# An inverse table permuted so that result stores take every third partition, and loads of a second transform ordered behind the chunks' transfers

## The chip, the core and the metric

The kernel runs on one core of one Trainium2 chip. TensorE (PE) multiplies matrices into PSUM, VectorE (DVE), ScalarE (ACT) and GpSimd (POOL) work on tiles in SBUF, whose first axis is the partition (0 to 127), and SyncE (SP) issues nearly all DMA transfers between SBUF and DRAM. Each engine takes its instructions in the order in which they were queued. The metric is the device time of one execution in microseconds, as the median of several runs.

## The reference

The input is x of shape (2, 3136, 256). Three blocks follow each other:

```
...
    X = np.fft.rfft(x, axis=1)
    Yr = Xr @ w_r - Xi @ w_i + b_r
    Yi = Xr @ w_i + Xi @ w_r + b_i
    Yr = np.sign(Yr) * np.maximum(np.abs(Yr) - lam, 0.0)   # Yi the same
    y = np.fft.irfft(Y, n=x.shape[1], axis=1)
...
    ch = np.maximum(xn @ w_ch1, 0.0) @ w_ch2               # xn: x normalised per row
    x = x + ch
...
    u = x + real(fft(fft(x, axis=1), axis=2))
    out = u + np.maximum(un @ w_ch1, 0.0) @ w_ch2          # un: u normalised per row
```

## The kernel before

The 3136 rows of a batch are split as 49 x 64 (n1 x n2), so that each Fourier transform along the rows is a 49-point one, a twiddled 64-point one, and back. The kernel has four stages.

The first transform, its mixing with w_r and w_i, the shrinking and the inverse 64-point part run as steps over both batches (`p2_b`, `p2_mix`, `p2_inv`). The result lies in `yg[b]`, one tile per batch with 128 partitions of 32 KB. Class `Inverse` does the inverse 49-point part with the table `cim`: `quad` (L336) multiplies with it, and the result is written back into `yg[b]`, with n1 as the partition, channel half h in partitions 64h to 64h + 48. `store(c)` writes it to DRAM (`dY`), rows n1 = 16c to 16c + 15 of each half in one DMA of 512 KB, 16 partitions of 32 KB; c = 3 is the one row left, n1 = 48. For batch 0 the order is: store piece 0, load the first two chunks' rows from dY, store pieces 1 to 3. For batch 1, pieces 0 and 1 are queued behind a transfer of the fourth chunk, and 2 and 3 behind one of the fifth (`store3`).

Then come 13 chunks of up to 512 rows of the first two-layer block (`mlp1`), and 13 of the second (`mlp2`), in `run_mlp`. A chunk's rows are fetched (L657), their mean and variance taken, normalised, turned in two steps by DVE (`flip`, L710) and a round trip through DRAM (dT<-q at L716, then `land`, q<-dT at L724), split by ACT and DVE or POOL into a high and a low part in tile u0r (`trans`), and multiplied: `l1` (PE L217 to L219, ACT L771, DVE L773), `l2` (PE L792 and L793, DVE adds L798 and L799), `store` (L808). The first two chunks are turned on PE instead (L748, then ACT L751). The tile u0r lies where `yg[0]` lay, so its first write waits until `yg[0]` has been stored. The first layer's matmuls, the second layer's and the other stages' all stand in one order on PE.

The transform along the rows for the third block (`Stage98`, "second transform") runs between the chunks, in eight steps per batch: batch 0 in chunks 8 to 10 of mlp1, batch 1 in chunks 1 to 3 of mlp2. `start` loads what the middle channel needs and the first two pieces, `ahead` a third, each of the first five steps one more. A piece is two DMAs of 256 KB (L398, u0r<-dX), written into a ring of four buffers; POOL folds it for batch 1 (L410 to L412), `quad` multiplies, ACT copies, SP stores it (dA<-o).

The order of instructions on each engine comes from a planner, which places them by modelled times and dependencies; the position in the source gives the priority. `tc.issue_after(ins)` adds the rule that what is traced inside it stands behind `ins` on `ins`'s engine. It orders and adds no semaphore.

Of the kernel before, what the change touches and what calls it, by code (L numbers as in the profile page):

```python
# [67 lines left out]
def _tables():  # L68


    t = {}

    def ang(num, den):
        return 2.0 * np.pi * (np.asarray(num, np.int64) % den) / den

    n1 = np.arange(N1)
    ca = np.zeros((NQ, NQ))
    cam = np.zeros((NQ, 4, 32))
    cim = np.zeros((4, 32, 64))

    for s in range(2):
        for k1 in range(1, NK + 1):
            a = ang(n1 * k1, N1)
            q = 4 * (k1 - 1) + s
            ca[2 * n1 + s, q] = np.cos(a)
            ca[2 * n1 + s, q + 2] = -np.sin(a)
            cam[2 * n1 + s, 2 * s, k1] = np.cos(a)
            cam[2 * n1 + s, 2 * s + 1, k1] = -np.sin(a)
            cim[2 * s, k1, n1] = np.cos(a)
            cim[2 * s + 1, k1, n1] = -np.sin(a)  # L90
        ca[2 * n1 + s, 96 + s] = 1.0
        cam[2 * n1 + s, 2 * s, 0] = 1.0
        cim[2 * s, 0, n1] = 1.0
    cs = ca.copy()
    for q in range(0, 96, 4):
        cs[:, q:q + 2], cs[:, q + 2:q + 4] = -ca[:, q + 2:q + 4], ca[:, q:q + 2]
    cq = np.zeros((128, 128))
    for s in range(2):
        cq[64 * s:64 * s + N1, 0:N1], cq[64 * s:64 * s + N1, 64:64 + N1] = ca[s::2, s::2], cs[s::2, s::2]
    t["ca"] = cq  # L100
    t["cam"] = cam.reshape(NQ, 128)
    t["cim"] = cim.reshape(128, 64)

    n2 = np.arange(N2)[:, None]
    k2 = np.arange(N2)[None, :]
    cb = np.zeros((2, N2, NK + 1, 128))
    ci = np.zeros((2, N2, NK, 2, N2))
    sg = np.where(np.arange(N2) >= 32, -1.0, 1.0)[None, :]
    for k1 in range(0, NK + 1):
        a = ang(n2 * (k1 + N1 * k2), N)  # L110
        c, s = np.cos(a), np.sin(a)
        re = np.stack([c, s])
        im = np.stack([-s, c])
        cb[:, :, k1, 0:32] = im[:, :, 32:]
        cb[:, :, k1, 32:96] = re
        cb[:, :, k1, 96:128] = im[:, :, :32]
        if k1:
            f = 2.0 / N
            ci[0, :, k1 - 1, 0] = f * c.T
            ci[1, :, k1 - 1, 0] = -f * (s * sg).T  # L120
            ci[0, :, k1 - 1, 1] = f * s.T
            ci[1, :, k1 - 1, 1] = f * (c * sg).T
    cb[:, :, 1:] = cb[:, :, 1:].reshape(2, 2, 32, NK, 128).swapaxes(0, 1).reshape(2, N2, NK, 128)
    t["cb"] = cb.reshape(128, (NK + 1) * 128)
    t["ci"] = ci.reshape(128, NK, 2, 2, 32).swapaxes(2, 3).reshape(128, NK * 128)

    kk = np.arange(33)[None, :]
    a = ang(n2 * (N1 * kk), N)
    cb0 = np.zeros((N2, 102))
    ci0 = np.zeros((68, N2))  # L130
    cb0[:, 0:33] = np.sin(a)
    cb0[:, 34:67] = np.cos(a)
    cb0[:, 68:101] = -np.sin(a)
    t["cb0"] = np.stack([cb0.reshape(2, 32, 102), np.zeros((2, 32, 102))], 1).reshape(128, 102)
    w = np.full((33, 1), 2.0 / N)
    w[0] = w[32] = 1.0 / N
    ci0[0:33] = w * np.cos(a).T
    wi = w.copy()
    wi[0] = wi[32] = 0.0
    ci0[34:67] = -wi * np.sin(a).T  # L140
    t["ci0"] = np.stack([ci0.reshape(68, 2, 32), np.zeros((68, 2, 32))], 2).reshape(68, 128)

    c = np.arange(D // 2)[:, None]
    kd = np.arange(129)[None, :]
    a = ang(c * kd, D)
    cd = np.stack([np.cos(a), np.sin(a)], 1)
    cd[0, 1, 0], cd[0, 1, 128] = 1.0, -1.0
    cd[1:, 1, 0] = cd[1:, 1, 128] = 0.0
    t["cd"] = cd.reshape(D // 2, 2 * 129)
    t["ident"] = np.eye(128)  # L150
    ident = t.pop("ident")
    out = {"ident": ident.astype(np.float32)}
    for k in ("ca", "cam", "cim", "cb", "ci", "cb0", "ci0", "cd"):
        out[k] = t.pop(k).astype(np.float32)
    assert not t
    return out
# [3 lines left out]
def fourier_moe_kernel(ctx, tc, x, w_r, w_i, b_r, b_i, g_ln, w11, w12, w21, w22,  # L160
                       t_ca, t_cam, t_cim, t_cb, t_ci, t_cb0, t_ci0, t_cd, t_ident, out):
    nc = tc.nc
    sp = nc.sync
# [37 lines left out]
    def v_copy(o, i):  # L201
        nc.vector.tensor_copy(o, i)

    mark, tab = {}, {}

    def sub(eng, o, a, b):
        ins = eng.tensor_tensor(out=o, in0=a, in1=b, op=ALU.subtract)
# [56 lines left out]
    yg = [cp.tile([128, 2, 32, 128], F32, tag=f"u{b}", name=f"yg{b}") for b in range(NB)]  # L264
# [23 lines left out]
    class Forward:  # L288
# [8 lines left out]
        def load(self, k, cut=1):  # L297
            t = self.slot()[0:NQ]
            w = 1024 // cut
            for e in range(cut):  # L300
                ins = sp.dma_start(out=t[:, e * w:(e + 1) * w],
                                   in_=x[self.b, k][:, e * w:(e + 1) * w])
                mark["sp"] = getattr(ins, "ins", ins)
            self.raw[k] = t
# [44 lines left out]
    class Inverse:  # L349
# [24 lines left out]
        def store(self, c):  # L374
            n0, n1 = 16 * c, min(16 * c + 16, N1)
            for h in range(2):
                v = yg[self.b][64 * h + n0:64 * h + n1].rearrange("p s j c -> p (s j c)")
                o = dY[self.b][h].rearrange("(n s) f -> n (s f)", s=2)[n0:n1]
                sp.dma_start(out=o, in_=v)

    class Stage98:
# [10 lines left out]
        def load(self):  # L392
            g = self.nl
            if g >= 8:
                return
            t = next(s98_ring)
            for s in range(2):
                sp.dma_start(out=t[64 * s:64 * s + 64], in_=self.src[s][:, g * 1024:(g + 1) * 1024])  # L398
            self.raw[g] = [t[:, e * 512:(e + 1) * 512] for e in range(2)]
            self.nl += 1  # L400

# [227 lines left out]
    class Chunk:  # L629
# [15 lines left out]
        def fetch(self):  # L645
            y = next(y_ring)
            if self.front is None:
                self.y = y.rearrange("p (h i c) -> p i h c", h=2, c=128)
            else:
                self.y = y.rearrange("p (i c) -> p i c", c=D)  # L650
            for ps_, i, n, ap in self.loads:
                if self.front is None:
                    o = y.rearrange("p (h i c) -> p h i c", h=2, c=128)[ps_, :, i:i + n, :]
                else:
                    o = self.y[ps_, i:i + n, :]
                    o = o if n > 1 else o[:, 0, :]
                ins = sp.dma_start(out=o, in_=ap)  # L657
                self.got = getattr(ins, "ins", ins)

        def like(self, a):  # L660
            return a if self.front is not None else a.rearrange("p (h c) -> p h c", h=2)
# [42 lines left out]
        def flip(self, h):  # L704

            x = self.nt * 32
            if h == 0:
                self.z = q_tiles[1]
            z = self.z[:, h * 4 * x:(h + 1) * 4 * x]
            nc.vector.transpose(out=z.rearrange("p (j i t) -> p i j t", j=4, t=32),  # L710
                                in_=self.yn[:, 0:self.nt, h * 128:(h + 1) * 128]
                                .rearrange("p i (j c) -> p i j c", j=4))
            if h == 0:
                return
            d = next(dT_ring).rearrange("h f -> (h f)")[0:1024 * x]
            ins = sp.dma_start(out=d.rearrange("(h p f) -> p h f", h=2, p=128),  # L716
                               in_=self.z[:, 0:8 * x].rearrange("p (h f) -> p h f", h=2))
            self.trip = getattr(ins, "ins", ins)
            self.d = d

        def land(self):
            x, d = self.nt * 32, self.d
            self.xt = q_tiles[2]
            ins = sp.dma_start(out=self.xt[:, 0:8 * x].rearrange("p (i x) -> p i x", i=8),  # L724
                               in_=bass.AP(d.tensor, d.offset, [[x, 128], [128 * x, 8], [1, x]]))
            self.trip = getattr(ins, "ins", ins)

        def trans(self, c):
            nt = self.nt
# [71 lines left out]
        def store(self, last):  # L801

            for ps_, i, n, ap in self.stores:
                if i + n - 1 != last:
                    continue
                s = self.o[ps_, i:i + n, :]
                eng = nc.scalar if self is mlp2[-1] and ps_.start == 64 else sp
                ins = eng.dma_start(out=ap, in_=s if n > 1 else s[:, 0, :])  # L808
                self.sent = getattr(ins, "ins", ins)

    ALLP = slice(0, 128)

# [230 lines left out]
    for i in range(NS + INV_BEHIND):  # L1043
# [6 lines left out]
        at = [inv0 if 2 * i + d in range(2 * STAGE3_FROM + 2, 2 * STAGE3_FROM + 10) else None for d in range(2)]  # L1050
# [37 lines left out]
    def run_mlp(chunks, nxt, hooks):  # L1088

        allc = chunks + nxt  # L1090
        for k, ch in enumerate(chunks):
# [17 lines left out]
            if n is not None and n.flipped:  # L1109
                if not n.landed:  # L1110
                    put(LAND_AT, land, n, allc[k - 1].sent if k else None)
                for c in range(2):
                    put(("l2", 0), split, c)
# [183 lines left out]
```

## Time and profile before

| | us |
|---|---|
| median of 3 runs | 799.08 (798.7 to 799.92) |
| the profiled execution | 795.47 |
| its span, first to last instruction | 793.7 |
| PE busy | 772.1 (97%) |
| DVE busy | 547.2 (69%) |
| ACT busy | 360.2 (45%) |
| POOL busy | 104.6 (13%) |

The profile is of one execution. Busy times of engines overlap, and the busy time of PE includes time at a lower clock. Of the 101.02 MB that DMA moves, 100.18 go through the one queue that SP feeds.

### The profile page before, as it was taken

How to read it: one execution, taken by the hardware profiler on the slowest of the kernel's cores; microseconds unless marked ns; L12 is line 12 of the kernel's file. 1: busy time of each engine (PE TensorE's matmuls, PEld its weight loads, DVE VectorE, ACT ScalarE, POOL GpSimd, SP SyncE). 2: the span in 40 equal slices, each digit the busy share in tenths (PEclk: the TensorE clock that was granted, in tenths of full speed). 3: DMA queues.
4: the chain of work that ended last, by engine and by line, in shares of the span. 5: the costliest groups of instructions: out<-in, count | busy, mean ns of one | idle time of the engine just before them, and what ended most of it. 6: DMA issues, size and time to landing. Idle time of an engine off the chain costs nothing.

```text
span 793.7 us, 12217 instructions
## 1 busy us (share of the span) xinstructions
PE 772.1 (97%) x4396; PEld 642.5 (81%) x4396; DVE 547.2 (69%) x1253; ACT 360.2 (45%) x791; POOL 104.6 (13%) x113
## 2 busy tenths in 40 slices
PE   9999999989999899999999999969999999999997
PEld 3989978966688789987778988757788898888887
DVE  6899986876755888867776766537556757666643
ACT  0553366356662444646443344346444435444421
POOL 0564312330110111100000001324100000000000
PEclk9999999999999999999999999989999999999999
DMA  8852204633087323495853227665543343322211
GB/s 244 247 184 111 81 1 54 163 111 107 27 222 189 105 92 107 153 222 160 264 171 99 88 85 172 179 178 156 151 137 92 107 124 121 109 70 73 62 34 40
DMA packets 84706, 101.02 MB, mean 127 GB/s; under 512 B 20306, under 2 KB 63036, under 8 KB 84450
## 3 DMA queue, kind: packets, MB, share of 16 engines
q1 hardware_dynamic: 84566, 100.18, 44.5%
q8 instruction: 35, 0.57, 0.3%
q14 instruction: 25, 0.20, 0.1%
q10 hardware_dynamic: 80, 0.07, 0.0%
HBM read 60.76 MB, written 41.42 MB: 129 GB/s over the span
## 4 chain that ended last, share of the span: by engine, by line
PE 83%; DMA 8%; DVE 5%; issue 1%; ACT 1%; SPq 1%; POOL 0%; ACTq 0%; DVEq 0%; POOLq 0%
PE psb L792 22%; PE psa L217 12%; PE psb L793 11%; PE psa L219 11%; PE psa L218 11%; PE psc L336 4%; PE psb L517 4%; DMA q<-dT 4%; DMA dY<-yg 3%; PE psc L862 3%; PE psa L484 1%; PE psc L887 1%; PE psa L323 1%; PE psc L539 1%; DVE yg L325 1%
## 5 line engine op out<-in xcount | busy, mean ns | idle before, releaser
L771 ACT ACTIVATE h<-psa 128x512 fp32r<-128x512 f32 (+2 forms) x208 | 117.9, 573 | 213.2 <-PE psa L219 160.4
L773 DVE SCALAR_TENSOR_TENSOR h<-psa,h 128x512 fp32r<-128x512 f32 (+2 forms) x208 | 135.0, 654 | 64.6 <-ACT h L771 60.7
L792 PE MATMUL psb<-r2b,h 128*128 128x512 f32 x392 | 138.1, 400 | 7.4 <-DVE o L799 7.4
L792 PE MATMUL psb<-r3a,h 128*128 128x512 f32 x392 | 137.7, 397 | 0.0
L793 PE MATMUL psb<-r3a,h 128*128 128x256 f32 x392 | 106.5, 280 | 0.0
L793 PE MATMUL psb<-r2b,h 128*128 128x256 f32 x392 | 106.4, 282 | 0.0
L792 PEld LDWEIGHTS psb<-r2b,h 128*128 128x128 f32 x392 | 72.6, 190 | 23.4 <-issue 8.2
L792 PEld LDWEIGHTS psb<-r3a,h 128*128 128x128 f32 x392 | 72.1, 188 | 21.0 <-issue 5.7
L217 PE MATMUL psa<-u0r,r3a 128*128 128x512 f32 (+1 forms) x208 | 81.4, 391 | 5.4 <-ACT u0r L199 3.4
L517 PE MATMUL psb<-wm,h 128*128 128x256 f32 (+1 forms) x600 | 84.4, 290 | 0.0
L217 PE MATMUL psa<-u0r,r2b 128*128 128x512 f32 (+2 forms) x208 | 82.0, 394 | 1.3 <-ACT u0r L199 1.3
L517 PEld LDWEIGHTS psb<-wm,h 128*128 128x128 f32 (+1 forms) x600 | 76.6, 188 | 5.0 <-issue 3.2
L218 PE MATMUL psa<-u0r,r3a 128*128 128x512 f32 (+1 forms) x208 | 79.4, 382 | 0.0
L218 PE MATMUL psa<-u0r,r2b 128*128 128x512 f32 (+2 forms) x208 | 78.7, 378 | 0.0
L219 PE MATMUL psa<-u0r,r2b 128*128 128x512 f32 (+2 forms) x208 | 78.3, 381 | 0.0
L793 PEld LDWEIGHTS psb<-r2b,h 128*128 128x128 f32 x392 | 74.8, 191 | 3.1
L219 PE MATMUL psa<-u0r,r3a 128*128 128x512 f32 (+1 forms) x208 | 76.7, 380 | 0.1
L793 PEld LDWEIGHTS psb<-r3a,h 128*128 128x128 f32 x392 | 73.9, 189 | 2.6
L798 DVE TENSOR_TENSOR o<-psb,yb 128x256 f32<-128x256 f32 x74 | 30.2, 421 | 65.5 <-PE psb L793 65.3
L199 ACT ACTIVATE yg<-psc 128x512 f32<-128x512 f32 (+1 forms) x58 | 48.2, 870 | 42.5 <-PE psc L539 28.0
L217 PEld LDWEIGHTS psa<-u0r,r3a 128*128 128x128 f32 x208 | 39.5, 190 | 19.6 <-issue 5.7
L217 PEld LDWEIGHTS psa<-u0r,r2b 128*128 128x128 f32 x208 | 39.1, 188 | 13.1 <-issue 5.7
(119 smaller groups left out, 1193.4 us busy)
## 6 DMA issues: line engine op xcount, KB each, us to landing
dT<-q SPq DMA_DIRECT2D x19, 512.0 KB
q<-dT SPq DMA_DIRECT2D x19, 512.0 KB
s<-in_moe_w_ch_dram SPq DMA_DIRECT2D x16, 512.0 KB
u0r<-dX SPq DMA_DIRECT2D x32, 256.0 KB
dA<-o SPq DMA_DIRECT2D x64, 128.0 KB
dY<-yg SPq DMA_DIRECT2D x12, 512.0 KB
r<-dA SPq DMA_DIRECT2D x48, 128.0 KB
dX<-o SPq DMA_DIRECT2D x10, 512.0 KB
```

The source lines that it names most:

```text
L199: nc.scalar.activation(out=o, in_=i, func=AF.Copy, scale=scale)
L217: nc.tensor.matmul(out=ps, lhsT=lh, rhs=rh, start=first, stop=False)
L218: nc.tensor.matmul(out=ps, lhsT=ll, rhs=rh, start=False, stop=False)
L219: ins = nc.tensor.matmul(out=ps, lhsT=lh, rhs=rl, start=False, stop=last)
L336: ins = nc.tensor.matmul(out=ps[s][64 * e:64 * e + 64, 0:n], lhsT=w[64 * s:64 * s + k], rhs=v[e][64 * s:64 * s + k], start=True, stop=True)
L517: ins = nc.tensor.matmul(out=ps[0:m, u * D:(u + 1) * D], lhsT=xv[:, o:o + m], rhs=wm_hl[wv][:, e, c, :], start=k == 0, stop=k == 11)
L771: ins = nc.scalar.activation(out=h[:, 0:n], in_=ps[:, 0:n], func=AF.Relu)
L773: ins = nc.vector.scalar_tensor_tensor(out=l[:, 0:n], in0=ps[:, 0:n], scalar=0.0, in1=h[:, 0:n], op0=ALU.max, op1=ALU.subtract)
L792: nc.tensor.matmul(out=ps, lhsT=h[:, ts_], rhs=w2[:, f, :], start=f == 0, stop=False)
L793: ins = nc.tensor.matmul(out=ps[:, 0:D], lhsT=l[:, ts_], rhs=w2[:, f, 0:D], start=False, stop=f == NF - 1)
L798: nc.vector.tensor_tensor(out=self.like(o), in0=self.like(ps[:, 0:D]), in1=self.y[:, i], op=ALU.add)
L862: nc.tensor.matmul(out=ps, lhsT=self.raw[p][0:n, k, q * 128:(q + 1) * 128], rhs=self.cols(n, pr[k][1], im), start=True, stop=True)
```

## The change

The table `cim` gets its columns in another order. Column `at` holds n1: n1 = 0 to 15 go to columns 0, 3, 6, ..., 45, the next 16 to 1, 4, ..., 46, the next to 2, 5, ..., 47, and n1 = 48 stays. The partition of the result is the column of the table, so `store(c)` now reads partitions c, c + 3, ..., 16 of them; DRAM gets the same rows at the same places. Besides, a dictionary `spx` remembers the last DMA of the chunks that was traced on SP (fetch, dT<-q, q<-dT, output store), and the loads of the second transform are traced behind it.

```diff
@@ _tables
+    at = np.where(n1 < 48, n1 % 16 * 3 + n1 // 16, n1)
...
-            cim[2 * s, k1, n1] = np.cos(a)
-            cim[2 * s + 1, k1, n1] = -np.sin(a)
+            cim[2 * s, k1, at] = np.cos(a)
+            cim[2 * s + 1, k1, at] = -np.sin(a)
...
-        cim[2 * s, 0, n1] = 1.0
+        cim[2 * s, 0, at] = 1.0
@@ fourier_moe_kernel
-    mark, tab = {}, {}
+    mark, tab, spx = {}, {}, {}
@@ Inverse.store
-                v = yg[self.b][64 * h + n0:64 * h + n1].rearrange("p s j c -> p (s j c)")
+                p = slice(64 * h + c, 64 * h + 48, 3) if c < 3 else slice(64 * h + 48, 64 * h + 49)
+                v = yg[self.b].rearrange("p s j c -> p (s j c)")[p]
@@ Stage98.load
-            for s in range(2):
-                sp.dma_start(out=t[64 * s:64 * s + 64], in_=self.src[s][:, g * 1024:(g + 1) * 1024])
+            with tc.issue_after(spx["ins"]):
+                for s in range(2):
+                    sp.dma_start(out=t[64 * s:64 * s + 64], in_=self.src[s][:, g * 1024:(g + 1) * 1024])
@@ Chunk.fetch
-                self.got = getattr(ins, "ins", ins)
+                self.got = spx["ins"] = getattr(ins, "ins", ins)
@@ Chunk.flip, Chunk.land
-            self.trip = getattr(ins, "ins", ins)
+            self.trip = spx["ins"] = getattr(ins, "ins", ins)
@@ Chunk.store
                 self.sent = getattr(ins, "ins", ins)
+                if eng is sp:
+                    spx["ins"] = self.sent
```

## Rows read from the trace of the kernel before

**Rows 1.** The page's busy table: us, share of the span, instructions.
```profile
PE 772.1 (97%) x4396; PEld 642.5 (81%) x4396; DVE 547.2 (69%) x1253; ACT 360.2 (45%) x791; POOL 104.6 (13%) x113
```

**Rows 2.** Waits of PE, longest first: us in total, times, longest us.
```profile
PE psb L792 <- DVE o L799: 7.4, 1, 7.4
PE psa L217 <- ACT u0r L199: 4.7, 2, 3.4
PE psa L217 <- ACT u0r L751: 2.0, 1, 2.0
```

**Rows 3.** Chain of waits, 125 to 180 (start us, us, what); then PE's timeline.
```profile
132.30 10.45 DMA dY<-yg
...
146.32 14.43 DMA dY<-yg
...
161.01 0.70 ACT u0r L751
...
157.71 1.04 PE L748 MATMUL psc<-ident,q 128*128 128x128 f32 x8
```

**Rows 4.** Busy time by stretch; the last two columns are DMA share, GB/s.
```profile
132.00:134.00 2.00, 2.00 (x17) 1.97 (x17) 1.40 (x4) 0.99 (x3) 0.00 (x0) 1.00 2.45 262
...
136.00:138.00 2.00, 2.00 (x19) 2.00 (x18) 2.00 (x6) 0.51 (x2) 1.73 (x1) 1.00 1.93 262
...
156.00:158.00 2.00, 2.00 (x16) 1.85 (x15) 1.97 (x6) 0.09 (x1) 0.98 (x1) 1.00 0.40 131
```

**Rows 5.** SP's timeline, 100 to 260: start us, us, line, transfer, count.
```profile
220.44 8.51 SPq L379 DMA_DIRECT2D dY<-yg  x4
231.79 5.91 SPq L657 DMA_DIRECT2D yb<-dY  x5
237.75 0.47 SPq L716 DMA_DIRECT2D dT<-q  x1
238.26 5.10 SPq L379 DMA_DIRECT2D dY<-yg  x4
...
247.17 4.06 SPq L724 DMA_DIRECT2D q<-dT  x1
```

**Rows 6.** Chain of waits, 240 to 275.
```profile
247.17 11.21 DMA q<-dT
...
260.64 0.79 PE psa L217
```

**Rows 7.** SP's timeline, 395 to 600.
```profile
487.64 9.68 SPq L398 DMA_DIRECT2D u0r<-dX  x10
...
501.26 0.83 SPq L716 DMA_DIRECT2D dT<-q  x1
...
510.03 0.57 SPq L808 DMA_DIRECT2D out_dram<-o  x1
510.70 0.70 SPq L724 DMA_DIRECT2D q<-dT  x1
```

**Rows 8.** DVE's timeline, 440 to 600: the turn and the last output add.
```profile
492.89 1.30 DVE L710 STREAM_TRANSPOSE q<-q 128x512 f32<-128x512 f32 x2 [1.33 <-ACT q L697]
...
498.55 0.42 DVE L799 TENSOR_TENSOR o<-psb,o 128x256 f32<-128x256 f32 x1
```

**Rows 9.** Chain of waits, 505 to 525.
```profile
510.70 7.66 DMA q<-dT
...
522.77 0.77 PE psb L792
```

**Rows 10.** Busy time by stretch: PE busy is third, granted clock third from last.
```profile
260.00:264.00 4.00, 3.36 (x8) 2.68 (x9) 3.87 (x7) 2.71 (x7) 2.91 (x2) 0.57 0.00 0
...
522.00:527.00 5.00, 4.23 (x14) 3.64 (x15) 2.26 (x5) 3.45 (x10) 0.00 (x0) 0.53 0.48 119
```

**Rows 11.** Chain of waits, 510 to 560: the quads of a step.
```profile
536.69 1.02 PE psc L336 x8
```

**Rows 12.** Waits of SP's queue: us in total, times, longest us.
```profile
SPq L716 <- DVE q L710: 43.4, 9, 21.5
```

More of the change, by code (lines that the diff above doesn't have):

```diff
@@ L725, in land @@
                                in_=bass.AP(d.tensor, d.offset, [[x, 128], [128 * x, 8], [1, x]]))
-            self.trip = getattr(ins, "ins", ins)
+            self.trip = spx["ins"] = getattr(ins, "ins", ins)
         def trans(self, c):
```

## The prediction

> **What bounds the kernel now.** I read the page's busy table first. TensorE (PE) is busy in 772.1 of 793.7 us [rows 1], so a change of transfers can only win back what is left, 21.6 us, and what the clock loses after a pause. The list of waits says where PE pauses: three waits carry 12.7 us [rows 2], 2.0 before the first chunk's first matmul (ACT u0r L751), 3.4 before a chunk's first layer (ACT u0r L199), and 7.4 in a second layer (DVE o L799). Each is then followed in the chain of waits and in SP's timeline, since all three end in a transfer that SP issued.
>
> First pause, 160 us. The inverse result of batch 0 is stored in four pieces. Piece 0 lands after 10.45 us; only then can the first chunk's rows be loaded, and pieces 1 to 3 are queued behind those loads and land 14.43 us after the last of these issues. The tile that the chunk's split data goes to lies on the stored one, so ACT L751 waits for the last store until 161.01 [rows 3], and PE idles 2.0 us [rows 2].
>
> Second pause, 258 us. Batch 1's pieces go out as four stores at 220.44 and four at 238.26; between them five loads wait for the first group. The chunk's turned data (q<-dT) is issued from 247.17 on, and the issue alone takes SP 4.06 us, a sign of full queues [rows 5]; it lands 11.21 us after it began. ACT's operations follow and PE starts at 260.64 [rows 6] after 3.4 us idle.
>
> Third pause, 515 us. SP issues ten loads of the second transform (u0r<-dX, 256 KB each) in one go at 487.64, 9.68 us in all. What follows is late: the turned tile is ready at 494.2 (DVE L710 at 492.89, 1.30 long), but dT<-q goes out at 501.26; the chunk's last output rows are added by 499.0 (L799 at 498.55), but their store is issued at 510.03, with q<-dT behind it at 510.70 [rows 7, 8]. That lands after 7.66 us. ACT splits the tile, DVE subtracts, and behind that subtraction in DVE's queue stand the L798 and L799 adds that free PSUM for PE, which restarts at 522.77 [rows 9] after 7.4 us idle.
>
> [...] All three with their clock are 2.0 + (3.4 + 1.7) + (7.4 + 2.0) = 16.5 us.
>
> **The change, part by part.** *Table and stores.* The table's columns are permuted and a store takes partitions c, c+3, c+6 and so on. It has the same instructions, the same 512 KB per store, the same 16 rows of 32 KB; the matmul reads a table of the same shape, so PE pays nothing. What changes is which rows travel together. In the stretch from 132 us one store's 16 rows begin together (262 GB/s x 2 us is 524 KB, one store) with a share of 2.45, so 2.45 x 2 = 4.9 us for a row (a transfer is booked where it starts, hence a share above 1). The other half's store, in the stretch from 136, has 1.93, or 3.9 us. In the stretch from 156, where pieces 1 to 3 have drifted apart, 262 KB (8 rows on 16 engines) carry 0.40, which is 0.40 x 2 x 2 = 1.6 us each [rows 4]. So a row mostly by itself needs 1.6 us and 16 neighbours in step need 4.9: neighbours share something. Every-third rows lie between 4.9 (nothing gained) and 1.6. I take 3.9, the price where rows are partly out of step: a fifth off each store.
>
> [...]
>
> At 160: piece 0 ends 1.8 us earlier (a fifth of 4.9 + 3.9), pieces 1 to 3 a fifth of 14.43 earlier, 2.9: together 4.7. Without the store ACT could start when PE's transposes allow, about 158.75 (157.71 + 1.04) [rows 3], 2.3 us earlier; half of the 4.7 would do. The 2.0 us go, hidden then by PE's last matmuls of the stage before. Gain 2.0; lower bound 0.
>
> At 258: the first group runs from 220.44 until the last loads behind it may go, about 235 (their issues end at 237.70). A fifth of 14.6 is 2.9. The next tile is turned no earlier, so dT<-q stays at 237.75 and the second group at 238.26 [rows 5], but it meets queues that are some 2.7 us emptier, and its own two large stores lose a fifth of 8.8, 1.8. q<-dT then lands at 258.4 - 4.5 = 253.9. For PE not to wait it has to land by 258.4 - 3.4 = 255.0: the pause goes, and the clock's 1.7 us with it. Gain 5.1; lower bound 0.
>
> *Loads behind the transfers.* The added context only orders SP's instructions; it is no semaphore. The two loads of start() (four DMAs) already stand behind the transfer traced before them and stay at 487. The load of ahead() goes behind dT<-q of the third chunk, that of the first step behind its q<-dT, that of the second step behind stores of outputs. So six DMAs leave their place ahead of dT<-q, two return between it and q<-dT, net four: 4 x 0.97 = 3.9 us of SP, and 1.05 MB out of the queues, 4.0 us at 262 GB/s [rows 4, 7]. These overlap, so I take 4.2 and not the sum: q<-dT lands at 514.2 in place of 518.4, PE restarts at 518.6, and 3.2 us of pause are left. Of the clock's 2.0 us I count half. Gain 5.2; bounds 0 (other issues take the room) and 9.4 (dT<-q at 494.2, q<-dT at 499, nothing ahead of it).
>
> What the moved loads may delay is the quads on PE. The fourth step's stand at 536.69 [rows 11]; its load is now issued right behind q<-dT, so after 510.70 at worst, 26 us ahead. Some 10 us go for landing and folding on POOL (an estimate from the 7.66 us of q<-dT), and 16 us of chunk matmuls remain as cover. The other steps' loads stand at similar distances, and I cost them at nothing; without cover each would be a pause of PE (rival F).
>
> Sum: 2.0 + 5.1 + 5.2 = 12.3 us. From the profiled execution, 795.47 (span 793.7 and 1.8 around it), that leaves 783.2; the median of the runs stands 3.6 higher, 799.08, and gives 786.8. Predicted 787.
>
> **Rivals.** B: q<-dT at 510 stays late. For it: of the 13.4 us between the ten loads' end and 510.70 SP fills nearly all with other issues [rows 7]. Against: six issues fewer ahead of dT<-q. Gain 2.0 + 5.1: 792.0.
>
> C: all pauses go. For it: dT<-q's 7 us behind its turn are pure order on SP. Against: the outputs' stores still go first. Gain 16.5: 782.6.
>
> D: every-third rows gain nothing (half of the change doesn't do what it says). Against: 4.9 beside 1.6 us [rows 4]. Only 5.2: 793.9.
>
> E: neither helps, another transfer is late in place of each: 799.
>
> F, slower: a load now stands behind a transfer that itself waits, SP and PE take their instructions in order, and PE stands at a quad. SP's longest wait for a turned tile is 21.5 us [rows 12]; with ten issues of 0.97 that is a hold of 31.2. The cover is 16, so PE would stand 15.2 us, 2.9 more than the sum: 802. It decides from a hold of 16 + 12.3 = 28 us. Against: no wait of that length stands in the list for these chunks' transfers.
>
> **How the numbers follow.** The forecast (A) has 0.47, B 0.16, C 0.10, D 0.09, E 0.08, F 0.10. A change within 0.2% (1.6 us) is about what a measurement of this kernel can't tell from none. Faster holds A to D, 0.82; same 0.08; slower 0.10. The likeliest case's own range is 784 to 790, since the order of all other instructions is planned anew too. The range of 8 in 10 takes in C (782.6) and D (793.9) with 1 to 2 us for that: 782 to 796. E and F lie outside.
>
> **What would show it.** Right: dY<-yg at 132 landing in under 9 us and no wait of PE on L751; q<-dT at 247 landing in under 8, no pause and clock 1.00 at 260; four, not ten, u0r<-dX in a row at 487, dT<-q some 5 us nearer to its turn, and PE's pause at 515 halved. Wrong: dY<-yg as slow as before; the room between turn and dT<-q filled by other issues; POOL's folds or the quads waiting for u0r<-dX; a new pause where none was.

## The result, and the profile after

The changed kernel takes 789.79 us (median of four runs, 789.01 to 790.71) where the kernel before takes 798.89 (four runs, 797.3 to 799.92): 9.1 us less, a ratio of 0.9888 with an interval of 0.9868 to 0.9908. It is faster, inside the predicted range and 2.8 us above the predicted 787. The profiled execution took 789.01 with a span of 787.1, 6.5 us less than before's 795.47 (6.6 of span). The other 2.6 us are where each profiled execution lies among its runs (before's 3.4 under its median, this one 0.8). The clock goes with that: in the runs below, executions of the kernel before at 794.7 to 796.4 us have a mean granted clock of 0.991 to 0.993, those at 799.2 and more one of 0.987 to 0.989, and the changed kernel's four have 0.992 to 0.994.

The same instructions stand in the same order on PE, DVE, ACT and POOL in both kernels. Only SP's order differs. So the n-th instruction of PE can be set against the n-th of before. By that, PE is 2.7 us ahead after the place of the first pause (0.1 of it from earlier), 8.0 after the second, 8.1 when the third begins, 7.0 by 522 and 6.6 from 552 to the end. Two pauses are gone, and the third has grown.

The busy table of the kernel after, and its waits of PE (us in total, times, longest), to be read against [rows 1, 2]:

```profile
PE 771.3 (98%) x4396; PEld 642.6 (82%) x4396; DVE 545.7 (69%) x1253; ACT 359.7 (46%) x791; POOL 104.4 (13%) x113
...
PE psb L795 <- DVE o L802: 7.8, 2, 7.7
PE psc L933 <- POOL wz L929: 1.1, 1, 1.1
PE psa L218 <- ACT u0r L200: 1.1, 1, 1.1
```

The lines have moved by one to three. L795, L802, L218 and L200 are before's L792, L799, L217 and L199, and the wait on before's L751 is off the list. SP's timeline from 100 to 260 answers to [rows 3, 5]:

```profile
131.66 1.22 SPq L381 DMA_DIRECT2D dY<-yg  x2
139.63 0.89 SPq L660 DMA_DIRECT2D stg<-dY  x2
...
217.73 7.24 SPq L381 DMA_DIRECT2D dY<-yg  x4
226.49 4.61 SPq L660 DMA_DIRECT2D yb<-dY  x5
234.73 0.36 SPq L719 DMA_DIRECT2D dT<-q  x1
235.14 4.16 SPq L381 DMA_DIRECT2D dY<-yg  x4
243.53 0.38 SPq L727 DMA_DIRECT2D q<-dT  x1
```

The load behind batch 0's first piece goes out at 139.63; before, that piece landed at 142.75 (132.30 + 10.45) and its load went out at 142.82. The loads behind batch 1's first group go at 226.49, not 231.79, and q<-dT is issued in 0.38 us where it took 4.06. Of before's four stores from 220.44 the first issue took 0.39 us and the fourth 4.48, so a short issue is read here as one with little unfinished ahead of it. ACT's timeline shows its rows used at 249.47, without a wait ahead of them:

```profile
249.47 1.33 ACT L743 ACTIVATE w<-q,g_sb 128x512 f32<-128x512 f32 x2
```

Busy time by stretch (columns as in [rows 4, 10]): at 132 the same store has a share of 1.42, so 1.42 x 2 = 2.84 us for a row, on average, where it had 4.9. From 252 to 256, where PE now does what it began at 260.64 [rows 6], its clock is 1.00. From 514 to 521 it is 0.52.

```profile
132.00:134.00 2.00, 2.00 (x16) 1.94 (x16) 1.64 (x4) 0.75 (x3) 0.00 (x0) 1.00 1.42 262
...
252.00:256.00 4.00, 4.00 (x22) 3.40 (x22) 4.00 (x8) 1.73 (x5) 2.96 (x2) 1.00 0.00 0
...
514.00:521.00 7.00, 6.02 (x19) 5.17 (x20) 2.96 (x8) 3.24 (x10) 1.24 (x3) 0.52 0.38 104
```

Around the third pause, SP's timeline answers to [rows 7], and the chain of waits to [rows 9]:

```profile
479.39 3.37 SPq L401 DMA_DIRECT2D u0r<-dX  x4
...
486.92 0.84 SPq L719 DMA_DIRECT2D dT<-q  x1
487.80 3.18 SPq L401 DMA_DIRECT2D u0r<-dX  x2
...
492.73 3.99 SPq L811 DMA_DIRECT2D out_dram<-o  x2
497.28 1.84 SPq L660 DMA_DIRECT2D yb<-dX  x2
499.37 0.56 SPq L811 DMA_DIRECT2D out_dram<-o  x1
```

```profile
500.03 10.12 DMA q<-dT
...
514.98 0.76 PE psb L795
```

DVE's timeline has the turn, to be read against [rows 8]:

```profile
484.80 1.31 DVE L713 STREAM_TRANSPOSE q<-q 128x512 f32<-128x512 f32 x2 [1.34 <-ACT q L700]
```

Four loads go out in a row, not ten. The tile is turned at 486.1, and dT<-q follows 0.8 us later, where it stood 7 us behind its turn. Set against the start of PE's pause (522.77 - 7.4 = 515.4 before, 514.98 - 7.7 = 507.3 after), q<-dT was issued 4.7 us ahead of it before and is issued 7.3 us ahead now: 2.6 us gained. But it lands after 10.12 us in place of 7.66 and gives 2.5 of these back. The stretches after its issue show that it is not short of room:

```profile
500.00:502.00 2.00, 2.00 (x13) 1.71 (x12) 1.93 (x7) 0.73 (x2) 1.24 (x4) 1.00 0.09 22
502.00:504.00 2.00, 2.00 (x13) 1.73 (x12) 0.88 (x3) 0.00 (x0) 1.32 (x3) 1.00 0.72 197
504.00:506.00 2.00, 2.00 (x13) 1.74 (x12) 0.00 (x0) 0.00 (x0) 0.00 (x0) 1.00 0.38 118
506.00:508.00 2.00, 1.31 (x11) 0.29 (x9) 0.00 (x0) 0.00 (x0) 0.00 (x0) 1.00 0.98 263
```

From 504 to 506 the DMA engines are 38% busy while the transfer that PE needs has not landed. What it waits for is some part of it, not bandwidth as a whole.

### The profile page after: what moved, and what is told of

It reads as the page before. It is cut to its first block, busy times and chain, and to the rows that moved or that the text cites. A ratio compares the mean times of both kernels' runs of the same rounds, so it can differ in the third digit from the quotient of the medians.

```text
span 787.1 us, 12213 instructions
## 1 busy us (share of the span) xinstructions
PE 771.3 (98%) x4396; PEld 642.6 (82%) x4396; DVE 545.7 (69%) x1253; ACT 359.7 (46%) x791; POOL 104.4 (13%) x113
## 4 chain that ended last, share of the span: by engine, by line
PE 88%; DMA 4%; DVE 4%; issue 1%; ACT 1%; SPq 1%; POOL 0%; DVEq 0%; POOLq 0%; ACTq 0%
PE psb L795 22%; PE psb L796 11%; PE psa L218 11%; PE psa L220 11%; PE psa L219 11%; PE psb L520 7%; PE psc L337 4%; DMA q<-dT 4%; PE psc L867 2%; PE psa L487 2%; PE psc L542 2%; PE psa L324 2%; PE psc L892 1%; DMA yb<-dX 1%; PE psc L933 1%
## 5 line engine op out<-in xcount | busy, mean ns | idle before, releaser
L795 PE MATMUL psb<-r2b,h 128*128 128x512 f32 x392 | 138.9, 401 | 7.8 <-DVE o L802 7.8
L795 PE MATMUL psb<-r3a,h 128*128 128x512 f32 x392 | 137.6, 397 | 0.0
L795 PEld LDWEIGHTS psb<-r2b,h 128*128 128x128 f32 x392 | 73.0, 191 | 24.2 <-issue 8.5
L795 PEld LDWEIGHTS psb<-r3a,h 128*128 128x128 f32 x392 | 72.1, 188 | 20.8 <-issue 5.7
L218 PE MATMUL psa<-u0r,r2b 128*128 128x512 f32 (+2 forms) x208 | 82.0, 394 | 1.1 <-ACT u0r L200 1.1
L218 PE MATMUL psa<-u0r,r3a 128*128 128x512 f32 (+1 forms) x208 | 80.5, 387 | 0.0
L200 ACT ACTIVATE yg<-psc 128x512 f32<-128x512 f32 (+1 forms) x58 | 48.1, 869 | 41.0 <-PE psc L542 26.5
L218 PEld LDWEIGHTS psa<-u0r,r3a 128*128 128x128 f32 x208 | 39.0, 188 | 13.4 <-issue 5.7
L218 PEld LDWEIGHTS psa<-u0r,r2b 128*128 128x128 f32 x208 | 39.1, 188 | 13.0 <-issue 4.9
```

The lines of the kernel that those rows point to most:

```text
L200: nc.scalar.activation(out=o, in_=i, func=AF.Copy, scale=scale)
L218: nc.tensor.matmul(out=ps, lhsT=lh, rhs=rh, start=first, stop=False)
L795: nc.tensor.matmul(out=ps, lhsT=h[:, ts_], rhs=w2[:, f, :], start=f == 0, stop=False)
```

## The experiments

Twelve kernels ran, in four jobs; the kernel before ran in each, at 798.58 to 799.95. Edits are made on the changed kernel.

| kernel | median us | ratio to before (interval) |
|---|---|---|
| e1_every_third | 788.77 | 0.9875 (0.9852 to 0.9898) |
| e2_order_alone | 799.12 | 1.0005 (0.9988 to 1.0022) |
| e3_no_mirrored_out, work left out | 783.0 | 0.9806 (0.9785 to 0.9827) |
| e4_no_straight_out, work left out | 786.97 | 0.9859 (0.9834 to 0.9884) |
| e5_turn_first | 788.35 | 0.9869 (0.9835 to 0.9903) |
| e6_turn_first_unordered | 786.6 | 0.9853 (0.9815 to 0.9891) |
| e7_every_fourth | 789.7 | 0.989 (0.9859 to 0.9921) |
| e8_fourth_turn_first | 788.35 | 0.9876 (0.9841 to 0.991) |
| e9_mirrored_on_act | 790.78 | 0.9888 (0.9855 to 0.9922) |
| e10_unordered_all | 792.37 | 0.9908 (0.9878 to 0.9938) |
| e11_ordered_all | 791.65 | 0.99 (0.9872 to 0.9929) |
| e12_first_loads_ordered | 784.1 | 0.9803 (0.9783 to 0.9822) |

### Each half of the change alone

**e1_every_third** keeps the stores and lets the loads go where they went before:

```diff
-            with tc.issue_after(spx["ins"]):
+            with ExitStack():
```

> The changed kernel without the ordering of the second transform's loads: the permuted table and the every-third stores alone. All engines but SP have the changed kernel's order, SP that of before. Theory: the stores alone remove the pauses at 160 and 258 us, which moved PE's start of the chunk behind them by 2.5 and 5.2 us between the two profiles, and the pause at 515 stays as it was before, 7.4 us with 2.0 us of clock. So 798.9 - 7.7 = 791.2, ratio 0.990, and a span of about 786. Rival (the prediction's sum, in which the ordering brings 5.2 us of its own): the stores alone are 5 us slower than the changed kernel, about 795, ratio 0.995.

**e2_order_alone** keeps the ordering and stores neighbouring partitions again:

```diff
-    at = np.where(n1 < 48, n1 % 16 * 3 + n1 // 16, n1)
+    at = n1
...
-                p = slice(64 * h + c, 64 * h + 48, 3) if c < 3 else slice(64 * h + 48, 64 * h + 49)
+                p = slice(64 * h + n0, 64 * h + n1)
```

> The changed kernel with the table and the stores of before: only the loads are ordered behind the chunks' transfers. The order on every engine is that of the changed kernel. Theory: in the changed kernel's profile the third pause is 7.7 us and the clock is low for longer behind it, so the ordering alone brings nothing: 799 to 800.5, ratio 1.000 to 1.002, and the pauses at 160 (2.0 us) and 258 (3.4 us) are back. Rival (the prediction): the ordering alone is worth 5.2 us, 793.7, ratio 0.9935, with a third pause near 3 us.

e1 takes 788.77, all of the change's gain. Waits of PE in e1: the pauses at 160 and 258 are gone and the third is as it was; its ten loads are back in SP's timeline, and the chain of waits has q<-dT issued late and landing quickly:

```profile
PE psb L795 <- DVE o L802: 7.3, 1, 7.3
```

```profile
480.62 9.68 SPq L401 DMA_DIRECT2D u0r<-dX  x10
```

```profile
503.65 7.74 DMA q<-dT
```

e2 takes 799.12, and its interval includes 1. Its waits of PE list all three pauses of before, and in its chain of waits the stores take before's time and q<-dT as long as in the changed kernel:

```profile
PE psb L795 <- DVE o L802: 7.8, 2, 7.4
PE psa L218 <- ACT u0r L200: 4.6, 3, 3.2
PE psa L218 <- ACT u0r L754: 1.9, 1, 1.9
```

```profile
132.00 10.44 DMA dY<-yg
...
145.74 14.60 DMA dY<-yg
...
510.61 9.90 DMA q<-dT
```

So the stores bring the whole gain, and the ordering is worth nothing that these runs can tell. It shifts time from SP's queue into the transfer.

The profiled execution of e2 took 799.82, close to the median of the kernel before, where before's own profile has one of its fastest. In it the clock falls behind the first pause too, and for longer behind the second (busy time by stretch):

```profile
161.00:165.00 4.00, 3.66 (x9) 2.61 (x10) 1.99 (x6) 1.91 (x5) 1.42 (x2) 0.60 0.81 280
...
261.00:268.00 7.00, 6.51 (x16) 5.11 (x17) 6.87 (x14) 4.27 (x10) 2.92 (x2) 0.53 0.21 74
```

That is 0.40 x 3.66 = 1.5 us and 0.47 x 6.51 = 3.1 us of PE's work lost, where before's profile has none and 1.7.

### What holds q<-dT

Two kinds of output rows go out between dT<-q and q<-dT: straight ones, 64 partitions at a time, and mirrored ones, which the program writes to DRAM as two blocks of 64 rows. The DMA view of the changed kernel from 480 to 515 lists six stores of one chunk, four of 64 KB and two of 128 KB, so the bytes of the two kinds are equal. Two straight stores, a mirrored one and a mirrored load (yb<-dX at 498.57) stand between dT<-q and q<-dT. **e3_no_mirrored_out** leaves out the mirrored output stores of one chunk, **e4_no_straight_out** the straight ones of the same chunk; neither writes those rows of the output.

```diff
-                if i + n - 1 != last:
+                if i + n - 1 != last or self is mlp2[0] and ps_ == ALLP:
```

(`ps_ != ALLP` in e4.)

> The changed kernel, but the first chunk of the second block leaves out its two stores of mirrored rows (128 KB each, DRAM side 2 x 64 x 256), so those rows of the output are not written. On SP one load of mirrored rows also comes to stand behind the third chunk's q<-dT. PE, DVE, ACT and POOL keep their order. Theory (mirrored rows hold it up): q<-dT of the third chunk is late because its last rows wait behind the mirrored stores and loads issued just ahead of it, so without three of these the pause of 7.7 us falls under 2.5 us, with little or no low clock after it: 5 to 9 us faster than the changed kernel, 781 to 785. Rival (SP's issues and the bytes set it, as the prediction had it): three issues of 0.5 us and 0.38 MB less, 1.5 to 2.5 us of the pause, which stays above 5 us; 787 to 788.

> The changed kernel, but the first chunk of the second block leaves out its four stores of straight rows (64 KB each, 64 x 256), so those rows of the output are not written; the mirrored stores and both loads of mirrored rows stay ahead of the third chunk's q<-dT. The control to the run without the mirrored stores: four issues and 0.25 MB less on SP against three and 0.38 MB. Theory (mirrored rows hold it up): q<-dT is issued some 2 to 4 us earlier but lands at most 2 us earlier, the pause stays at 5.5 to 7.7 us, 787 to 790. Rival (SP's issues and the bytes set it): the pause shrinks by as much as in the other run or more, 2 to 4 us, to about 4, and the time to 785 to 787.

e3 takes 783.0 and has no pause near 515. SP's timeline, then ACT's: q<-dT is issued at 496.26, and ACT, which names no wait, splits it from 502.38. It landed in 6.1 us at the most. The mirrored load stands behind it in this kernel, at 496.99, so no mirrored rows are left ahead of it.

```profile
496.26 0.38 SPq L727 DMA_DIRECT2D q<-dT  x1
```

```profile
502.38 1.14 ACT L200 ACTIVATE u0r<-q 128x512 fp32r<-128x512 f32 x2
```

e4 takes 786.97. q<-dT is issued 0.8 us later than in e3, takes 9.26 us, and PE pauses for 3.3 us. Its chain of waits, then ACT's and PE's timelines:

```profile
497.05 9.26 DMA q<-dT
```

```profile
506.33 1.15 ACT L200 ACTIVATE u0r<-q 128x512 fp32r<-128x512 f32 x2 [4.51 <-DMA q<-dT]
```

```profile
511.13 0.77 PE L795 MATMUL psb<-r2b,h 128*128 128x512 f32 x1 [3.32 <-DVE o L802]
```

With the same bytes of output taken away, the landing is 9.26 us behind mirrored rows and 6.1 or less without them (e3 also has the load's 128 KB behind it). Mirrored rows in the queue are what holds the transfer. The number of issues ahead counts too: e4's pause is 3.3 us and not 7.7, less than its theory allowed, because q<-dT went out 3 us earlier.

The traces also show which part of the transfer is late. They keep the times at which a transfer's semaphore is counted up; the last count is its landing, as the chain of waits has it (before's q<-dT: 510.70 + 7.66 = 518.36), and each count is taken here for a part of the transfer. Every dT<-q, q<-dT and straight row transfer of the second block has 16 counts. Each of the 24 mirrored loads and 24 mirrored stores has three: one soon after its issue (1 us, in one case 2.8) and two, at most 0.5 us apart, when it lands. For the third chunk's q<-dT (us from the span's start):

| kernel | mirrored rows right ahead, landed | issued | first 14 counts by | last two |
|---|---|---|---|---|
| before | load 514.40, store 516.87 | 510.70 | 514.87 | 518.35, 518.36 |
| changed | load 505.10, store 507.85 | 500.03 | 505.15 | 509.86, 510.15 |
| e4 | load 501.49, store 504.05 | 497.05 | 502.02 | 505.79, 506.31 |
| e3 | none | 496.26 | 500.20 | 500.21, 500.45 |

Behind mirrored rows, 14 of the 16 parts land in 4.2 to 5.1 us, and two land 3.5 to 5.0 us later, 1.5 to 2.3 us behind the mirrored store. Without them all 16 land in 4.2 us. The changed kernel's dT<-q, issued at 486.92 behind a mirrored store and load, has the same: 14 counts by 492.19 and the last two at 497.21 and 497.27, behind the load's 496.21.

A mirrored transfer has two counts at its landing, and a transfer of 16 behind it has two late ones. What ties the two to each other is not shown: the counts name no cause.

### The tile ahead of the outputs

If the stores ahead of it hold q<-dT, it should go first. **e5_turn_first** drops, for the second block, the rule that `land` stands behind the previous chunk's last store:

```diff
-                    put(LAND_AT, land, n, allc[k - 1].sent if k else None)
+                    put(LAND_AT, land, n, None if ch in mlp2 else allc[k - 1].sent if k else None)
```

**e6_turn_first_unordered** has this and e1's edit.

> The changed kernel, with the rule taken away that a chunk of the second block's q<-dT stands behind the last output store of the chunk before. Nothing is left out. PE, DVE, ACT and POOL keep their order; on SP the third chunk's q<-dT moves ahead of six transfers, among them one load and one store of mirrored rows. Theory: the pause at 515 is the landing of this transfer and nothing else, so it goes (under 1 us, no low clock) and the time is that of the run without the mirrored stores, 783, or up to 2 us less or more: 781 to 785. Rival: the transfer is late because dT<-q before it lands late or because the queues are full whatever is issued ahead; then 787 to 790 and a pause above 5 us.

> Every-third stores, the second transform's loads not ordered (ten in a row again, as before), and the rule on q<-dT taken away as in the run with the turn first. Other engines keep their order. Theory: the ordering of the loads is worth something only where the transfer behind them is not held up by mirrored rows; here q<-dT follows dT<-q, which still follows ten loads, so it is issued some 5 us later than with the loads ordered and PE pauses 1 to 4 us: 784 to 787, 1 to 4 us slower than the run with the turn first. Rival: the ordering of the loads is worth nothing at all; both within 1 us.

e5 misses its 781 to 785 with 788.35. The pause at 515 is gone, and one of 5.7 us stands 30 us later, in front of the fourth chunk. PE's timeline, and SP's:

```profile
545.93 0.80 PE L218 MATMUL psa<-u0r,r2b 128*128 128x512 f32 x1 [5.67 <-ACT u0r L200]
```

```profile
523.09 0.37 SPq L719 DMA_DIRECT2D dT<-q  x1
...
524.40 1.58 SPq L401 DMA_DIRECT2D u0r<-dX  x2
...
532.82 1.70 SPq L401 DMA_DIRECT2D u0r<-dX  x2
534.62 3.00 SPq L464 DMA_DIRECT2D dA<-o  x4
537.66 0.59 SPq L727 DMA_DIRECT2D q<-dT  x1
```

The third chunk's q<-dT goes out at 499.60, 0.4 us ahead of the changed kernel's, and lands in 4.63 us in place of 10.12, its 16 counts within 1.1 us. The fourth chunk's tile was turned at 511.9, and its q<-dT goes out at 537.66, behind late loads of the second transform, which the ordering had put there. Its granted clock is 0.67 from 545 to 552, so the new pause costs 5.7 + 0.33 x 6.07 = 7.7 us (PE is busy for 6.07 of that stretch), most of what the removal of the old one had gained (7.7 and the 2.9 of clock worked out below).

e6 takes 786.6, in its own 784 to 787, but was to be slower than e5 and is not (intervals overlap). Its ten loads are back ahead of the tile, and the chain of waits shows the other side of the exchange: dT<-q lands slowly, q<-dT quickly, with no output store between the two. The ten loads are not what makes dT<-q slow: 13 of its 16 parts have landed by 499.61, and the last two land at 502.88 and 502.90, behind a mirrored load that stands right ahead of it and lands at 501.61. PE pauses for 4.9 us, and nowhere later:

```profile
494.17 8.73 DMA dT<-q
...
502.97 4.16 DMA q<-dT
```

**e12_first_loads_ordered** is e5 with only the pieces up to the fifth ordered, so that the last three may go early:

```diff
-            with tc.issue_after(spx["ins"]):
+            with tc.issue_after(spx["ins"]) if g < 5 else ExitStack():
```

> The run with the turn first (ordered loads, q<-dT free of the rule on the last output store), but of the second transform's loads only the third to fifth of each batch are ordered behind the chunks' transfers; the last three are not, and SP issues them right behind the first step's stores. Nothing is left out; the other engines keep their order. Theory (the ordering moved the last loads in between the fourth chunk's dT<-q and q<-dT and so made the pause of 5.7 us at 546): that pause falls below 3 us, the one at 515 stays away, and the time is 2 to 6 us below the run with the turn first, 782 to 786. Rival (the fourth chunk's transfers are late by their outputs and mirrored rows, wherever the loads stand): the pause stays at 4 to 6 us and the time at 787 to 789.

It takes 784.1, 15.2 us less than the kernel before in the same job (799.31), and 5.7 less than the changed kernel. SP's timeline has the last loads gone by 521, and the fourth chunk's q<-dT 3.6 us earlier than in e5; the waits of PE have no pause above 2.7 us, and busy time by stretch shows the clock behind that pause:

```profile
519.73 1.12 SPq L401 DMA_DIRECT2D u0r<-dX  x2
...
534.09 0.98 SPq L727 DMA_DIRECT2D q<-dT  x1
```

```profile
PE psc L867 <- ACT o L200: 2.7, 1, 2.7
PE psa L218 <- ACT u0r L200: 1.6, 1, 1.6
```

```profile
528.00:536.00 8.00, 7.17 (x27) 4.87 (x28) 5.62 (x19) 4.78 (x13) 4.27 (x9) 0.57 0.57 144
```

So with the last loads let go, e5's pause in front of the fourth chunk is gone, and e12 beats both kernels. How much of the pause went by q<-dT is less clear. It lands at 543.04, 2.2 us earlier than in e5 (545.22). PE also came to the chunk later, which hid the rest of the 5.7 us: it had paused for 2.7 us at 528, behind an ACT that waited for a store of the second transform (dA<-o), and lost 0.43 x 7.17 = 3.1 us of clock after it.

### How far apart rows must be

**e7_every_fourth** spreads a store's rows further; **e8_fourth_turn_first** adds e5's edit.

```diff
-    at = np.where(n1 < 48, n1 % 16 * 3 + n1 // 16, n1)
+    at = n1 % 16 * 4 + n1 // 16
...
-                p = slice(64 * h + c, 64 * h + 48, 3) if c < 3 else slice(64 * h + 48, 64 * h + 49)
+                p = slice(64 * h + c, 64 * h + 64, 4) if c < 3 else slice(64 * h + 3, 64 * h + 4)
```

> The changed kernel with the table's rows placed so that each store takes every fourth partition of 64 instead of every third of 48. Same instructions and order. [...]

> Every-fourth stores, ordered loads and the turn first together, nothing left out. Theory: every-fourth stores add nothing to the turn first, 781 to 785, within 1 us of it. Rival: emptier queues bring another 1 to 3 us.

Busy time by stretch of e7, the store at 132 again:

```profile
132.00:134.00 2.00, 2.00 (x18) 1.95 (x17) 1.46 (x4) 0.93 (x3) 0.00 (x0) 1.00 1.21 262
```

1.21 x 2 = 2.42 us for a row. So the mean is 4.9 us for neighbours, 2.84 for every third partition and 2.42 for every fourth. The slowest row of that store, by the trace's packets, took 5.06, 3.84 and 2.58 us. The time of the kernel stays at 789.7, since every third had already removed the two pauses. e8 takes what e5 takes: it meets the expected agreement with e5 and misses, as e5 does, the time below 785.

The slowest row falls by 1.22 us from neighbours to every third and by 1.26 from there to every fourth. The rows of that store are nearly alike as neighbours (4.72 to 5.06 us) and far apart as every third (1.65 to 3.84), so the mean there, 2.84, lies 1 us under the slowest. Which partitions hold each other up is not shown: the packets name none.

### The mirrored rows on another queue

**e9_mirrored_on_act** has ACT issue the mirrored output stores; **e10_unordered_all** adds e1's and e5's edits, **e11_ordered_all** adds e5's.

```diff
-                eng = nc.scalar if self is mlp2[-1] and ps_.start == 64 else sp
+                eng = nc.scalar if (ps_.start == 64 if self is mlp2[-1] else self.front is not None and ps_ == ALLP) else sp
...
-                self.sent = getattr(ins, "ins", ins)
                 if eng is sp:
+                    self.sent = getattr(ins, "ins", ins)
                     spx["ins"] = self.sent
```

> The changed kernel with the second block's output stores of mirrored rows (2 x 64 x 256) issued by ACT on its own queue and not by SP. Nothing is left out, the bytes are the same; ACT and SP are planned anew around them, and PE and DVE in places. On SP one load of mirrored rows comes to stand behind the third chunk's q<-dT. Theory (rows that wait in the one SP queue behind mirrored rows): dT<-q and q<-dT no longer stand behind those stores, q<-dT of the third chunk lands in 4 to 7 us, the pause at 515 goes below 3 us, and the time to 781 to 786. Rival (the engines or the bytes hold it up, whichever queue they come by, or SP's issues alone): 787 to 790 with a pause above 4 us. ACT's own waits before such a store (each waits for the DVE add) could cost some of it: a pause of PE on ACT h would show that.

> Every-third stores, loads of the second transform not ordered, q<-dT free of the rule on the last output store, and the mirrored output stores by ACT. Nothing is left out. PE keeps the changed kernel's order. Theory: dT<-q still follows the ten loads but no mirrored store, so it lands in 4 to 6 us and not 8.7 as in the run with the turn first and unordered, the pause of 4.9 us there goes below 2.5 and no later one replaces it: 781 to 785. Rival: the ten loads ahead of dT<-q are what holds it up, then the pause stays at 4 to 5 us and the time at 786 to 788.

> The same with the loads ordered behind the chunks' transfers, as in the changed kernel. Theory (the ordering moves the loads into the next chunk's stretch, where they delay its dT<-q and q<-dT): no pause at 515, but one of 1 to 6 us before the fourth chunk's first layer at about 540, as in the run with the turn first, so 782 to 788 and not faster than the run with the loads unordered. Rival (the ordering helps once the mirrored stores are out of the way): 2 to 4 us faster than unordered.

All three miss, at 790.78 to 792.37. In each the pause at 515 is gone, and PE waits elsewhere instead, in e9 for 5.7 us (its waits of PE):

```profile
PE psc L337 <- DVE w L900: 5.7, 1, 5.7
```

The order on ACT and DVE is planned anew once ACT issues transfers, so these kernels change more than the queue. They don't tell whether the mirrored rows would hold q<-dT from another queue; that stays open. In all three, q<-dT of the third chunk, with no mirrored rows right ahead of it in either queue, lands in 4.2 to 4.6 us, and dT<-q, with a mirrored load still ahead of it on SP, has its last two counts 4.3 to 5.0 us behind the other 14.

## Why the prediction was right, and where it was not

**First pause.** The mechanism held, and the term was 2.0 for 2.6 measured. The mean row cost 2.84 us and not 3.9, so the stores ended earlier than forecast (the load behind the first piece went out 3.2 us earlier and not 1.8). The slowest rows took 3.84 for 5.06. Half would have done, as the prediction said; that is why e7's shorter rows add nothing.

**Second pause.** 5.1 forecast, 5.3 measured (8.0 - 2.7), with the pause and the low clock both gone. Of the forecast, 1.7 is the clock's: 0.43, what the granted clock lacked, over 4 us [rows 10]. One step was wrong without harm: dT<-q did not stay at 237.75. It went at 234.73, since DVE turned the tile 2.7 us earlier (L713 at 233.41, where L710 was at 236.12), as far as PE and with it the other engines were ahead from the first pause; the loads, 5.3 us earlier, no longer stood in its way.

**Third pause.** 5.2 forecast; 1.5 us were lost (8.1 - 6.6). What the prediction says of SP came true: four loads in a row, and dT<-q next to its turn. The step that failed is "4 x 0.97 = 3.9 us of SP, and 1.05 MB out of the queues, 4.0 us", from which q<-dT was to land 4.2 us earlier. It took the landing to move with the issue, as if freed issues and bytes were what the transfer waited for. At 500 to 502 the share of DMA is 0.09, so full queues are not what it waited for. What it waited for, e3, e4 and the counts show: two of its 16 parts, which land only behind the mirrored rows, a load and an output store, that stand in the queue right ahead of it. The same happens to dT<-q, which the prediction's bound of 9.4 us let land in under 5 us (issued at 494.2, q<-dT at 499). Before, it took 8.7 us and landed at 509.96, only 0.7 us ahead of q<-dT's issue; in the changed kernel it took 10.35 us, its last two parts 5 us behind the others. So SP's other issues were not all that kept q<-dT late. With 2.6 us gained on SP and 2.5 lost in the landing the pause stayed, at 7.7 us for 7.4, and the clock after it took 0.48 x 6.02 = 2.9 us where it took 0.47 x 4.23 = 2.0 [rows 10], the forecast's figure for it: together 1.2 of the 1.5.

**The rivals.** It came out as B: q<-dT stays late and the stores' two terms remain. B reckoned 788.4 for the profiled execution (795.47 - 7.1), and that took 789.01. B's reason, SP filled with other issues, is not the right one, since the issue did move. D (the stores gain nothing) is refuted by e2 beside e1, C (all pauses go) by the pause itself. F's long hold of SP did not come. But e5 has a case of E's kind, a pause in place of a pause, of which the prediction spoke only in general.

**Total.** The sum was 12.3 and the traces show 6.6 of span. The medians differ by 9.1, so the forecast lies closer to the median (787 for 789.79) than the sum to its parts. That is in part luck, as two misses work against each other. The stores' two terms, 7.1 in the forecast, are worth 9.85 in e1 (798.62 to 788.77); the prediction took the clock from one execution and counted none behind the first pause, and in e2's, which is nearer to the median, the clock costs 1.5 us there and 3.1 behind the second. The ordering, 5.2 in the forecast, is worth nothing in e2.

What stays open: where e2's longer low clock comes from, and whether mirrored rows hold a transfer of another queue. Mirrored rows split into more than two parts were not tried.

## What to carry to other kernels

Stores of 16 rows of 32 KB gained here by being spread over the partitions (slowest row 5.06, 3.84 and 2.58 us), by a table that was there anyway and with the same instructions on PE; check that something waits for the store, since the step to 2.58 left the time at 789.7. Reordering issues moved a transfer's start here (2.6 us), and not its landing relative to PE (2.5 of these given back): look at what stands right ahead of it in its queue, at the DMA share while it is under way, and at when each of its parts lands. And when a pause goes, look one round later, at what the same reordering has put there.

## What was not expected of the hardware

- The mean price of a 32 KB row in a store of 16 partitions fell from 4.9 to 2.84 us by taking every third partition and to 2.42 by every fourth; the slowest row, which ends the store, from 5.06 to 3.84 and 2.58.
- A 512 KB transfer took 4.16 us with no output store between it and dT<-q (e6), 4.19 without mirrored rows ahead (e3), 9.26 with them and no straight ones (e4), and 10.12 with both, at a DMA share of 0.09 just after its issue. In the last two, 14 of its 16 parts had landed after 5.0 and 5.1 us.
- The issue of one such transfer took SP 4.06 us behind the stores of neighbouring partitions (before, 247.17) and 0.38 behind those of every third (changed, 243.53).
- After pauses of nearly the same length (7.4 and 7.7 us) the granted clock was 0.67 over 7 us in the one case (522 to 529, of which [rows 10] shows five) and 0.52 over 7 us in the other; after e5's 5.7 us pause it was 0.67 over 7 us as well.
